# A fused attention and SwiGLU kernel: block 0's output projection moved between block 1's steps, its weights loaded later and in pieces, and two more head pairs turned by DMA

## The chip, the cores and the metric

The kernel runs on one core of one Trainium2 chip. The metric is the time of one execution in device microseconds. The profile takes one execution apart. PE is TensorE (matmuls; PEld are its weight loads), DVE is VectorE, ACT is ScalarE, POOL is GpSimd and SP is SyncE. POOL and SP also issue the DMAs: POOL those that convert float32 in device memory to float16 in SBUF (queue q0), SP the DMA transposes and the stores of the result (queue q1).

## The reference

Attention over 8 batches of 12 heads, 448 tokens each, 64 wide, and then a gated feed-forward network over the 3584 tokens, whose 768 features are the heads side by side:

```python
scores = (q @ k.transpose(0, 1, 3, 2)) / np.sqrt(64)
attn = exp(scores - max(scores));  attn = attn / sum(attn)
x = (attn @ v).transpose(0, 2, 1, 3).reshape(3584, 768)
g, val = x @ w_gate, x @ w_val            # 768 x 1536 each
out = (g * sigmoid(g) * val) @ w_out      # 1536 x 768
```

q, k, v, the weights and the result are float32.

## The kernel before, in words

**Attention.** Two heads are one pair; six pairs are a batch, 48 pairs in all. For each pair the kernel loads q and k (`load_qk16`), brings them into the layout with the feature dimension on partitions (`prep`, giving the tile `qkT`), multiplies them in four units of keys (`qk`, tile `s` in PSUM), lets ScalarE take the exponential (tile `E`), multiplies that with v (`pv`, tile `acc`), and lets VectorE divide by the sums that come along as a 65th column (tile `R`, tile `xt`). `xt` is then turned into the columns of `X` (`turn_x`). v is loaded by `load_v`, three pairs at a time for the first twelve, and copied into its place with the column of ones by VectorE (`copy_v`, tile `vo`).

There are two ways to lay out q and k. Pairs below `NPE` are turned on TensorE by 18 transposing matmuls (the inner function `turn` of `prep`, tile `tp`) and copied out by VectorE. From `NPE` on, POOL copies q and k into the tile `qk16` (three buffers) and SP issues two DMA transposes into `qkT`. Pairs from `QUAD` = 12 on are of another layout with 128 keys to a unit and always go by DMA. For `turn_x`, pairs below `XPE` = 12 use TensorE (tile `xtp`) and a copy by VectorE.

**Feed-forward network.** The tokens come in blocks: block 0 has 384 tokens, block 1 has 512 and so on. A step (`Step`) is one of 12 slices of 128 columns of the gate and value weights: six matmuls for the gate (`gate`, tile `gp`), a tanh on ScalarE (`sg`), a product on VectorE (`gated`, tile `t`), six matmuls for the value (`value`, tile `vp`) and a last product (`finish`, tile `hts`). Weights lie in four parts each (`wg`, `wv`; three steps use one part). The output projection of block 0 is plain: six products of 12 matmuls with 384 columns (`plain_out`, run one at a time by `run_o`, tile `op`), with weights `wo` in two halves, evicted by ScalarE and stored by SP. Later blocks use sums of the weights that VectorE builds from `wo` (`out_sums`), which save matmuls.

**The order.** All instructions are written out by hand in program order (`manual_schedule`), and each engine runs its own in that order. After the first six pairs, whose order is a list of strings, the loop over `plan` makes visits: each visit issues two or three score units, then the products of pairs that are complete (`todo`), and then steps of the network. The number of units is two up to pair `WIDE` and three from there on. How many steps a visit gets is decided in three ways: for the first 12 visits by a budget (`run_budget`, `left`, `carry`), which spreads what is left of the current block by its matmul time up to the next block, for the seven visits ahead of `base` by the list `FIRST_STEPS`, and after that by the table `VISITS`. A turn of `xt` stands at the end of its visit (`turns`). v for the products of a visit is copied one visit earlier (`vcopies`).

**Loads.** `wq` says which loads are emitted when a pair is entered: for example `4: [("g", 3), ("v", 3), ("qk", 12)]` and `6: [("V", 3), ("o", 0)]`. POOL issues them in order. Every DMA has one of eight semaphores in turn, so an issue waits until the DMA eight issues before it has landed. A copy or matmul waits for the semaphores of the loads that it reads.

**PSUM.** The pool `ps_f` has two buffers of one bank (`acc`, `vp`, `xtp` and, in some visits, `gp`), the pool `ps_s` three of two banks (`s`, most `gp`). Buffers are handed out in turn, so an allocation waits for the readers of the one two (or three) before it.

The functions that the change touches:

Of the kernel before, what the change touches and what calls it, by code (L numbers as in the profile page):

```python
# [10 lines left out]
FP32 = mybir.dt.float32  # L11
# [7 lines left out]
GP = 3  # L19
NPE = 12  # L20
LA = 6
RS = 8
RL = 4
FIRST = 6
WIDE = 8
XPE = 12
# [6 lines left out]
QUAD = 12  # L33
# [31 lines left out]
def kernel(  # L65
# [10 lines left out]
    nc = tc.nc  # L76
    B, H, S, D = q.shape
    DM = H * D
    DF = moe_w_gate.shape[1]
# [140 lines left out]
    def load_w(kind, i):  # L220
        if kind == "o":
            src = moe_w_out[:, ts(i, OH)].rearrange("(f p) m -> p f m", p=128)
            dst = wo[i]
        else:
            src = (moe_w_gate if kind == "g" else moe_w_val)[:, ts(i, DF // 4)].rearrange(
                "(t a p) m -> t p a m", p=128, t=2
            )
            for t in range(2):
                nc.gpsimd.dma_start(wgv[kind, i][:, ts(t, NCB // 2), :], src[t])
            return  # L230
        nc.gpsimd.dma_start(dst[:], src)

# [241 lines left out]

    def turn_x(pr):
        b, hp = divmod(pr, NHP)
# [5 lines left out]
        if pr < XPE:  # L482
            tp = accs[pr] if pr < FIRST else ps_f.tile([128, 512], FP32, tag="f", name="xtp")
            for j in range(3):
                nc.tensor.matmul(
                    tp[:, ts(j, 128)],
                    lhsT=xt[:, 2 * j : 2 * j + 2].rearrange("p h d -> p (h d)"),
                    rhs=ident[:],
                    start=True,
                    stop=True,  # L490
                )
            nc.vector.tensor_copy(dst[:, 0:MQ], tp[:, 0:MQ])
            return
# [387 lines left out]
    with tc.manual_schedule():  # L881
# [6 lines left out]
        for vo in Vts:  # L888
# [20 lines left out]
            3: [("qk", 9, 1), ("qk", 10), ("g", 2), ("v", 2)],  # L909
            4: [("g", 3), ("v", 3), ("qk", 12)],  # L910
            6: [("V", 3), ("o", 0)],
            8: [("o", 1)],
        }
# [30 lines left out]

        def add_block(i, visits):
            if i < B - NB - 1:
# [26 lines left out]

        FIRST_STEPS = [2, 2, 1, 2, 1, 1, 1]
        VISITS = [
            (2, 2, 0, 0, 2), (0, 2, 0, 0, 3), (0, 1, 1, 0, 0), (0, 2, 0, 0, 0), (0, 1, 1, 0, 0),
            (0, 2, 0, 0, 0), (0, 1, 1, 0, 0), (0, 2, 0, 0, 0), (0, 1, 1, 0, 0), (3, 2, 0, 0, 1),
            (0, 2, 0, 0, 1), (0, 1, 1, 0, 0), (0, 0, 0, 1, 0), (0, 2, 0, 0, 0), (0, 0, 0, 1, 0),
            (0, 1, 1, 0, 0), (0, 0, 0, 1, 0), (0, 2, 0, 0, 0), (0, 0, 0, 1, 0), (0, 2, 0, 0, 0),
            (4, 2, 0, 0, 1), (0, 2, 0, 0, 1), (0, 1, 1, 0, 0), (0, 1, 0, 0, 0), (0, 1, 1, 0, 0),  # L980
            (0, 1, 0, 0, 0), (0, 1, 1, 0, 0), (0, 1, 0, 0, 0), (0, 1, 1, 0, 0), (0, 1, 0, 0, 0),
            (5, 0, 0, 1, 0), (0, 0, 0, 2, 0), (0, 0, 0, 0, 0),
        ]
# [28 lines left out]

        def run_fv(quiet=False):
            step = fvq.pop(0)
            step.gate()
            step.value(0)
            if not quiet:
                add_sum()
            step.finish()
            if not quiet:  # L1020
                add_sum()
            return 2 * step.time

        def run_pair():
# [30 lines left out]
        def run_o():  # L1055
            gen, t = oq.pop(0)
            next(gen)
            if len(oq) < 2 and not groups and wsums:
                n = 3 if oq else 4
                sums.extend(wsums[:n])  # L1060
                wsums[:n] = []
                add_sum(n)
            return t

# [29 lines left out]
        def run_two_groups(inside=None):  # L1094
            gens = [groups.pop(0)[0]() for _ in range(2)]
            for stage in range(2):
                for gen in gens:
                    next(gen)
                if inside and not stage:
                    inside()  # L1100

        def run_budget(budget):
            while (fvq or oq) and budget > 0:
                if not fvq:
                    budget -= run_o()
                elif len(fvq) > 1 and gate_small[0] and 2 * fvq[0].time < budget:
                    budget -= run_pair()
                elif len(fvq) > 1 and fvq[0].at[1] and 2 * fvq[0].time < budget <= 4 * fvq[0].time:
                    budget -= run_pair()
                else:  # L1110
                    budget -= run_fv(bool(fvq[0].at[1]))
            return budget

        def left():
            return sum(2 * step.time for step in fvq) + sum(t for _, t in oq)

        def share(total, at, n):
            return (at + 1) * total // n - at * total // n

# [56 lines left out]
        turns = []  # L1176

        def open_products(rests):
            for p0 in rests:
                pv_open(p0)  # L1180
                pv_rest(p0)
            return []
# [3 lines left out]

        carry = 0.0
        after_group = False
# [6 lines left out]
        for x, (chunks, todo) in enumerate(plan):  # L1195
# [13 lines left out]
            open_products(rests)  # L1209
            if x == 2:  # L1210
                turn_rests(0)
            end = min([y for y in adds if y > x] + [len(plan) + 1])
            if x == 0:
                add_block(0, end)
            early = [p0 for p0 in vcopies.get(x, []) if p0 < QUAD or x > base]
# [3 lines left out]
            for pr in entered:  # L1219
                lead = [pr + 3] if pr + 3 < QUAD else [pr + 3, pr + 4] if pr + 3 == QUAD else [pr + 4]  # L1220
                for p in lead:
                    if NPE <= p < NPAIR:
                        prep(p)
# [7 lines left out]
            if x in adds and 0 < x < base:  # L1231
                add_block(adds[x], end - x)
            around = bool(todo) and x > base and VISITS[x - base][1:3] == (0, 1)
# [12 lines left out]
            bare = not todo and bool(chunks) and x > 0  # L1246
            if 0 < base - x <= len(FIRST_STEPS):
                n = FIRST_STEPS[x - base]
                gate_small[0] = bare
                if n > 1:  # L1250
                    run_pair()
                else:
                    run_fv(True)
            elif x < base:
                if bare and oq and not fvq:
                    carry -= run_o()
                elif bare:
                    gate_small[0] = True
                out_small[0] = not fvq and bool(oq) and any(p0 >= QUAD for _, p0 in todo)
                extra = 2 * fvq[0].time if bare and len(chunks) == 3 and fvq and not fvq[0].at[1] else 0  # L1260
                carry = run_budget(left() / (end - x) + carry + extra) - extra
            else:
                begins, nf, ng, no, ns = VISITS[x - base]
                gate_small[0] = bare
                if begins > 2:
                    add_block(begins, 0)
                after_group = ng > 0
# [15 lines left out]
                if begins == 2:  # L1283
                    add_block(2, 0)
                ahead = {3: (x + 1, x + 2), 2: (), 1: ()}.get(len(VISITS) + base - x, (x + 1,))
# [71 lines left out]
        p0 = NPAIR - 1  # L1357
        pv_open(p0, True)
        pv_rest(p0)
        pv_quad(p0)  # L1360
# [89 lines left out]
```

## Time and profile before

| | us |
|---|---|
| median of 3 runs (430.68 to 431.16) | 430.89 |
| the profiled execution | 429.48 |
| its span, first to last instruction | 427.7 |
| TensorE busy | 420.7 |
| VectorE, ScalarE, GpSimd busy | 268.8, 245.2, 233.3 |

The lines of the profile give the engine, the kernel's line, the operation, what is written and read, and how often; in a time line the first two numbers are start and length in us, and the bracket at the end is the engine's idle time just before and what ended it. TensorE's matmuls overlap in these lines (the end of one is modelled), so the start of the next line tells how long a group took. A view of windows gives for each stretch its length, the busy time of PE, PEld, DVE, ACT and POOL with the number of instructions, the granted clock as a share of full speed, the DMA engines' busy share and GB/s. In the view of DMA queues the columns are packets, MB and the packets' time as a share of 16 engines; in that of DMA issues the last columns are the count, the size in float16 and the median time from issue to landing.

### The profile page before, as it was taken

How to read it: one execution, taken by the hardware profiler on the slowest of the kernel's cores; microseconds unless marked ns; L12 is line 12 of the kernel's file. 1: busy time of each engine (PE TensorE's matmuls, PEld its weight loads, DVE VectorE, ACT ScalarE, POOL GpSimd, SP SyncE). 2: the span in 40 equal slices, each digit the busy share in tenths (PEclk: the TensorE clock that was granted, in tenths of full speed). 3: DMA queues.
4: the chain of work that ended last, by engine and by line, in shares of the span. 5: the costliest groups of instructions: out<-in, count | busy, mean ns of one | idle time of the engine just before them, and what ended most of it. 6: DMA issues, size and time to landing. Idle time of an engine off the chain costs nothing.

```text
span 427.7 us, 11618 instructions
## 1 busy us (share of the span) xinstructions
PE 420.7 (98%) x4639; PEld 291.0 (68%) x4639; DVE 268.8 (63%) x641; ACT 245.2 (57%) x395; POOL 233.3 (55%) x356
## 2 busy tenths in 40 slices
PE   8999999999999999999999999999999999999995
PEld 4666666655557777757666677777889985555795
DVE  4676572765669665575535786677777755665662
ACT  6976667546755654656666546559654235455221
POOL 8756543988978673577744876925998000000001
PEclk9999999999999999999999999999999999999999
DMA  9999999999999999999999998813101240000124
GB/s 137 179 201 200 200 178 169 127 175 178 154 147 130 127 152 147 142 157 120 130 157 120 160 149 94 138 37 95 23 1 39 76 123 27 0 0 2 38 85 138
DMA packets 107527, 49.77 MB, mean 116 GB/s; under 512 B 59840, under 2 KB 104208, under 8 KB 107472
## 3 DMA queue, kind: packets, MB, share of 16 engines
q0 software_dynamic: 46944, 24.83, 52.9%
q1 hardware_dynamic: 60384, 24.02, 33.6%
q8 instruction: 36, 0.59, 0.6%
q14 instruction: 19, 0.16, 0.1%
q10 hardware_dynamic: 144, 0.17, 0.1%
HBM read 49.55 MB, written 11.01 MB: 142 GB/s over the span
## 4 chain that ended last, share of the span: by engine, by line
PE 84%; DMA 8%; ACT 4%; issue 1%; DVE 1%; POOL 1%; SPq 0%; DVEq 0%; POOLq 0%
PE og L676 18%; PE gp L554 16%; PE vp L554 12%; PE un L792 10%; PE acc L420 8%; PE ub L792 8%; PE s L329 5%; ACT E L367 4%; DMA wo<-in_moe_w_out_dram 4%; DMA qkraw<-in_k_dram 3%; PE op L647 2%; DMA qkT<-qk 1%; PE s L341 1%; PE wp L163 1%; PE op L1000 1%
## 5 line engine op out<-in xcount | busy, mean ns | idle before, releaser
L349 ACT ACTIVATE E<-s 128x896 f16<-128x896 f32 x126 | 106.6, 918 | 40.3 <-PE s L329 28.4
L237 POOL COPY qk<-qkraw 128x512 f16<-128x512 f16 x72 | 45.3, 670 | 53.9 <-DMA qkT<-qk 48.8
L554 PE MATMUL gp<-X,wg 128*128 128x384 f16 (+1 forms) x360 | 73.8, 347 | 0.0
L554 PE MATMUL vp<-X,wv 128*128 128x384 f16 (+3 forms) x360 | 67.7, 324 | 0.0
L607 DVE SCALAR_TENSOR_TENSOR t<-sg,gp 128x384 f32<-128x384 f32 (+1 forms) x60 | 36.3, 607 | 43.0 <-ACT sg L581 42.7
L554 PEld LDWEIGHTS <-wv 128*128 128x128 f16 x450 | 42.9, 98 | 26.0
L637 POOL DMA_DIRECT2D out_dram<-osb x3 | 1.6, 539 | 90.9 <-ACT osb L695 90.9
L554 PEld LDWEIGHTS <-wg 128*128 128x128 f16 x360 | 32.8, 98 | 26.1 <-issue 1.9
L177 POOL DMA_DIRECT2D qkraw<-in_k_dram x70 | 43.0, 637 | 9.4 <-DMA wo<-in_moe_w_out_dram 5.8
L581 ACT ACTIVATE sg<-gp 128x384 f32<-128x384 f32 (+1 forms) x60 | 31.9, 537 | 27.6 <-PE gp L554 26.8
L420 PEld LDWEIGHTS <-E 128*128 128x128 f16 (+1 forms) x1152 | 39.0, 96 | 10.3 <-issue 2.5
L367 ACT ACTIVATE E<-s 112x896 f16<-112x896 f32 x48 | 40.2, 934 | 9.5 <-PE s L359 9.5
L676 PEld LDWEIGHTS <-hts 128*128 128x128 f16 x528 | 44.1, 98 | 0.4
L420 PE MATMUL acc<-vo,E 128*128 128x65 f16 (+1 forms) x1152 | 43.6, 193 | 0.2
L177 POOL DMA_DIRECT2D vraw<-in_v_dram x72 | 43.1, 613 | 0.0
L200 POOL DMA_DIRECT2D qkraw<-in_q_dram x44 | 30.5, 693 | 11.2 <-DMA wo<-in_moe_w_out_dram 6.7
L613 DVE SCALAR_TENSOR_TENSOR hts<-t,vp 128x384 f16<-128x384 f32 (+3 forms) x60 | 32.9, 548 | 5.6 <-PE vp L554 1.9
L695 ACT ACTIVATE osb<-og 128x384 f32<-128x384 f32 x22 | 10.8, 491 | 39.4 <-PE og L676 39.4
L450 DVE TENSOR_TENSOR xt<-acc,R 128x256 f16<-128x256 f32 x72 | 30.6, 425 | 2.5
L329 PE MATMUL s<-qkT 64*128 64x448 f16 x216 | 29.7, 353 | 0.0
L676 PE MATMUL og<-wo,hts 128*128 128x192 f16 x264 | 29.0, 246 | 0.0
L676 PEld LDWEIGHTS <-hsum 128*128 128x128 f16 x300 | 25.5, 98 | 1.0
(179 smaller groups left out, 722.3 us busy)
## 6 DMA issues: line engine op xcount, KB each, us to landing
vraw<-in_v_dram POOLq DMA_DIRECT2D x72, 64.0 KB, 4.0
qkraw<-in_q_dram POOLq DMA_DIRECT2D x41, 112.0 KB, 4.6
qkraw<-in_k_dram POOLq DMA_DIRECT2D x68, 64.0 KB, 4.8
wg<-in_moe_w_gate_dram POOLq DMA_DIRECT2D x8, 288.0 KB, 9.7
wv<-in_moe_w_val_dram POOLq DMA_DIRECT2D x8, 288.0 KB, 10.1
wo<-in_moe_w_out_dram POOLq DMA_DIRECT2D x2, 1152.0 KB, 18.2
out_dram<-osb SPq DMA_DIRECT2D x7, 288.0 KB, 3.8
out_dram<-osb SPq DMA_DIRECT2D x6, 336.0 KB, 3.2
```

The lines of the kernel that those rows point to most:

```text
L177: eng.dma_start(dst[ts(s, 64)], rows)
L237: nc.gpsimd.tensor_copy(dst.rearrange("p c h d -> p h c d"), src)
L329: nc.tensor.matmul(s[:, hx, 0:S], lhsT=t[ts(hx, 64), ts(c + low(pr, hx), 128)], rhs=t[ts(hx, 64), ds(NC * 128, S)], start=True, stop=True,)
L349: nc.scalar.activation(e[:, 0 : 2 * S].rearrange("p (h q) -> p h q", h=2), s[:, :, 0:S], AF.Exp, scale=sm_scale)
L367: nc.scalar.activation(e[:, :, 0:S], s[0:P, :, 0:S], AF.Exp, scale=sm_scale)
L420: nc.tensor.matmul(acc[:, ts(j, D + 1)], lhsT=e[rows, ds(hx * S + j * 128, 128)], rhs=Vts[pr % NV][rows, hx, col, 0 : D + 1], start=first, ...
L554: nc.tensor.matmul(dst[:, 0:w], lhsT=wslice(kind, self.fb, cb), rhs=X[kk][:, cb, ds(c0 + lo, w)], start=(cb == 0), stop=(cb == NCB - 1),)
L581: self.readers = [nc.scalar.activation(self.sg[:, 0:n], gp[:, 0:n], AF.Tanh, scale=0.5)]
L607: nc.vector.scalar_tensor_tensor(self.t1[:, 0:n], self.sg[:, 0:n], 1.0, self.gp[:, 0:n], ALU.add, ALU.mult)
L613: nc.vector.scalar_tensor_tensor(self.hts[:, self.fb, ds(lo, w)], self.t1[:, ds(lo, w)], 0.5 * HS, vp[:, 0:w], ALU.mult, ALU.mult)
L676: nc.tensor.matmul(dst, lhsT=lhs(n), rhs=rhs(n), start=first and n == 0, stop=n == NH - 1, skip_group_check=True)
L792: mm = nc.tensor.matmul(dst, lhsT=lhs[:, n], rhs=rhs[:, n], start=first and n == 0, stop=n == NK - 1, skip_group_check=True,)
```

## The change

1. The output projection of block 0 is moved: its six products no longer stand together in visits 8 to 11, but one each in visits 10, 11, 13, 14, 16 and 17, from visit 11 on inside a step of block 1 (`run_fv_with_o`), between the step's gate and its value, which is then made in two halves.
2. `wo` is loaded when pairs 10 and 12 are entered, instead of 6 and 8, and each half in two pieces of six slices.
3. `NPE` is 10 instead of 12: pairs 10 and 11 are turned by DMA. Which pairs are prepared when is told by a new table, `LEAD`. The load of q and k of pairs 12 and 13 stands ahead of the last quarter of gate and value weights.
4. A table, `FIRST_VISITS`, gives the number of steps and of projection products for each of the first 18 visits, in place of the budget and `FIRST_STEPS`. `WIDE` is 7 instead of 8, so there is one visit less in all, and `VISITS` is written anew: the same 33 entries in another order, but for two single projection products at the end in place of one visit with two and one with none. Block 0's twelve steps are spread over visits 0 to 9.
5. In visits with one step, the turn of `xt` stands inside the step, in the middle of its value group (`run_fv(..., with_turns)`), instead of behind all steps.
6. The last pair's leftover products are issued one visit earlier, and the sums for the later projections are taken two per visit from visit 13 on.

```diff
-NPE = 12
+NPE = 10
-WIDE = 8
+WIDE = 7
...
     def load_w(kind, i):
         if kind == "o":
-            src = moe_w_out[:, ts(i, OH)].rearrange("(f p) m -> p f m", p=128)
-            dst = wo[i]
+            src, n, dst = moe_w_out[:, ts(i, OH)], NFB, wo[i]
         else:
...
+            src, n, dst = (moe_w_gate if kind == "g" else moe_w_val)[:, ts(i, DF // 4)], NCB, wgv[kind, i]
+        src = src.rearrange("(t a p) m -> t p a m", p=128, t=2)
+        for t in range(2):
+            nc.gpsimd.dma_start(dst[:, ts(t, n // 2), :], src[t])
...
-            4: [("g", 3), ("v", 3), ("qk", 12)],
-            6: [("V", 3), ("o", 0)],
-            8: [("o", 1)],
+            4: [("qk", 12), ("g", 3), ("v", 3)],
+            6: [("V", 3)],
+            10: [("o", 0)],
+            12: [("o", 1)],
...
-        FIRST_STEPS = [2, 2, 1, 2, 1, 1, 1]
+        FIRST_VISITS = [
+            (1, 0), (1, 0), (1, 0), (2, 0), (1, 0), (1, 0), (1, 0), (2, 0), (1, 0), (1, 0), (0, 1),
+            (1, 1), (2, 0), (1, 1), (1, 1), (2, 0), (1, 1), (2, 1),
+        ]
...
-        def run_fv(quiet=False):
+        def run_fv(quiet=False, with_turns=False):
             step = fvq.pop(0)
             step.gate()
+            tp = ps_f.tile([128, 512], FP32, tag="f", name="xtp") if turns and with_turns else None
             step.value(0)
+            if tp:
+                step.gated()
+                turn_x(turns.pop(0), tp)
...
+        def run_fv_with_o(quiet):
+            step = fvq.pop(0)
+            step.split = step.alone = True
+            step.gate()
+            step.gated()
+            out_small[0] = True
+            run_o()
+            step.value(0)
+            step.finish()
+            if not quiet:
+                add_sum()
...
+        LEAD = {6: [], 7: [], 8: [10, 11], 9: [12], 10: [13, 14]}
...
             open_products(rests)
-            if x == 2:
+            if (NPAIR - 1, KR - 1) in chunks:
+                pv_open(NPAIR - 1, True)
+                pv_rest(NPAIR - 1)
+            if x == 1:
                 turn_rests(0)
...
-                lead = [pr + 3] if pr + 3 < QUAD else [pr + 3, pr + 4] if pr + 3 == QUAD else [pr + 4]
+                lead = LEAD[pr] if pr in LEAD else [pr + 4]
...
-            if 0 < base - x <= len(FIRST_STEPS):
-                n = FIRST_STEPS[x - base]
+            if x < base:
+                nf, no = FIRST_VISITS[x]
                 gate_small[0] = bare
...
+                if no and not nf:
+                    out_small[0] = True
+                    run_o()
+                elif no:
+                    for _ in range(nf - 1):
+                        run_fv(quiet)
+                    run_fv_with_o(quiet)
+                elif nf > 1:
                     run_pair()
                 else:
-                    run_fv(True)
...
+                    run_fv(quiet, not bare)
+                after_group = no > nf
+                if x > 12:
+                    add_sum(2)
```

## The prediction

> **What bounds the kernel now.** I read the page's busy shares first, then the chain of waits, then the time lines of TensorE, VectorE and GpSimd between 24 and 90 us, where the order of work changes, and the landing times of the loads there.
>
> ```profile
> PE 420.7 (98%) x4639; PEld 291.0 (68%) x4639; DVE 268.8 (63%) x641; ACT 245.2 (57%) x395; POOL 233.3 (55%) x356
> ...
> DMA  9999999999999999999999998813101240000124
> ```
>
> TensorE is busy for 98% of the span, so a microsecond for which it stands still is a microsecond of time. The DMA digits (a slice is 10.7 us) are full up to 256 us: loads come as fast as they can, and their order decides when each lands. The queue that GpSimd feeds, in 35 to 50 us, and then both queues in 57 to 68 us, when DMA transposes have joined:
>
> ```profile
> q0 software_dynamic: 4445, 2.97, 133.3%
> ...
> q0 software_dynamic: 2062, 1.41, 90.5%
> q1 hardware_dynamic: 1970, 0.48, 42.7%
> ```
>
> Alone, the loads (q0) get 4445/15 = 296 packets per us; beside transposes (q1) both get about the same, 187 and 179. So transposes cut the loads to 0.63 of their rate.
>
> The loads that matter, on GpSimd's time line (q and k of pair 9, then v of pairs 9 to 11, then the copies ahead of two pairs' transposes), and their times from issue to landing, from the DMA view of those moments:
>
> ```profile
> 26.36 0.68 POOL L200 DMA_DIRECT2D qkraw<-in_q_dram  x1 [1.03 <-DMA wv<-in_moe_w_val_dram]
> 27.80 0.66 POOL L200 DMA_DIRECT2D qkraw<-in_k_dram  x1 [0.77 <-DMA vraw<-in_v_dram]
> 44.46 0.78 POOL L211 DMA_DIRECT2D vraw<-in_v_dram  x1 [1.13 <-DVE hts L613]
> 52.66 2.28 POOL L237 COPY qk<-qkraw 128x512 f16<-128x512 f16 x4 [0.24 <-DMA qkraw<-in_k_dram]
> ```
> ```profile
> qkraw<-in_k_dram POOLq DMA_DIRECT2D x1, 112.0 KB, 7.9
> vraw<-in_v_dram POOLq DMA_DIRECT2D x1, 336.0 KB, 9.7
> qkT<-qk SPq DMA_TRANSPOSE x1, 8.9
> ```
>
> Pair 9's k lands at 27.80 + 7.9 = 35.7 us; v of pairs 9 to 11 at 44.46 + 9.7 = 54.2. Who needs them, on the time lines of TensorE and VectorE:
>
> ```profile
> 40.80 0.63 PE L302 MATMUL tp<-ident,qkraw 112*64 112x112 f16 x18
> 55.81 0.36 PE L385 MATMUL acc<-vo,E 112*128 112x65 f16 x6
> 56.79 1.14 PE L554 MATMUL gp<-X,wg 128*128 128x384 f16 x6
> 83.22 0.38 PE L341 MATMUL s<-qkT 64*64 64x448 f16 x3 [0.29 <-DMA qkT<-qk]
> ```
> ```profile
> 55.08 0.29 DVE L218 COPY vo<-vraw 112x512 f16<-112x512 f16 x1
> 56.99 0.20 DVE L404 RECIPROCAL R<-acc 128x7 f32<-128x7 f32 x1 [0.41 <-PE acc L393]
> 57.23 0.62 DVE L406 TENSOR_TENSOR xt<-acc,R 128x448 f16<-128x448 f32 x1
> ```
>
> At 40.80 pair 9 is turned, 5.1 us after its k is there. At 55.08 VectorE copies pair 9's v, only 0.9 us after it landed. 55.81 to 56.79 are pair 8's products, and the two rows that follow on VectorE normalise them. At 83.22 stands one of the two waits of TensorE that the profile lists (1.0 and 0.3 us); the other is at the start.
>
> **The change, part by part.** *Moved: block 0's projection and block 1's steps.* The table gives seven steps of block 0 to the first six visits, where the rule gave ten. The work is the same, but pairs now come earlier, while their loads keep their place in a full queue. Up to v of pairs 9 to 11 the queue's content is the same: q and k of pairs 12, 13 pass the last gate and value weights, nothing leaves it, and wo stood behind it anyway. GpSimd issues against landings (the bracketed releasers), not against TensorE. So that v still lands at 54.2 or later.
>
> First wait: the built order of the changed program has pair 9's turn in visit 2. Ahead of it, of what ran before 40.80, three steps are missing (1.95 + 3.90 us), pair 6's products and turn (0.98 + 0.26) and a score unit (0.2): TensorE is there at 40.8 - 7.3 = 33.5 and waits for 35.7, that is 2.2 us.
>
> Second wait: pair 9's v is copied a visit earlier, in visit 5, ahead of pair 8's normalisation in VectorE's order. Ahead of pair 8's products, of what ran before 55.81, four steps are missing (45.64 to 49.54 and 50.55 to 54.46: 7.81 us), the turns of pairs 10 and 11 (0.57 + 0.56) and a score unit (0.2). The products end at 56.79 - 9.1 = 47.7, and the next gate group (0.97) at 48.6, without the first wait. The value group behind it takes the PSUM buffer that pair 8's products hold, so it needs VectorE, which stands at the copy with the normalisation, the gate's product and the next turn's copy queued behind it. ScalarE then runs dry too, as its scores come from TensorE; GpSimd and SP go on.
>
> When does that v land now? GpSimd's copies of pairs 10, 11 (four, 2.3 us) follow its issue at once, so SP starts their transposes near 46.5. Before, the first transpose was issued at 53.30, took 8.9 us to land and has no packet in 50 to 57 us; by that delay of 3.7 us the new ones start at 50.2. The 4.0 us of loads left then take 4.0/0.63 = 6.3: landing at 56.5. Bounds: 54.2 if transposes take nothing, 57.5 if they start at once at 48.5. I take 56.5, as the window of 57 to 68 us is just this mixture. From landing to TensorE: 0.2 to the copy (an estimate; the released steps in the brackets above start within 0.6), 0.29 copy, 0.22 reciprocal with its gap, 0.62 product, 0.1: 1.4 us. TensorE goes on at 57.9 instead of 48.6: **+9.3 us**, the first wait included (bounds 7.0 and 10.3).
>
> *The clock.* TensorE then stands still from 50.8 to 57.9. At the end of the kernel, TensorE's last matmul ends at 422.7, and the granted clock of the next windows is
>
> ```profile
> 422.70:425.70 3.00, 0.00 (x0) 0.00 (x0) 0.36 (x1) 0.03 (x1) 0.00 (x0) 1.00 0.57 177
> 425.70:427.70 2.00, 0.00 (x0) 0.00 (x0) 0.00 (x0) 0.00 (x0) 0.00 (x0) 0.50 0.10 33
> ```
>
> so it halves 3.0 us into a pause. At the start it comes back late:
>
> ```profile
> 0.99 3.38 PE L163 MATMUL wp<-warm 128*128 128x512 f16 x8 [0.99 <-DVE warm L883]
> ...
> 5.19 0.61 PE L163 MATMUL wp<-warm 128*128 128x512 f16 x1
> ...
> 6.30 0.39 PE L163 MATMUL wp<-warm 128*128 128x512 f16 x1
> ```
>
> The matmul at 5.19 is still long, that at 6.30 is not: 4.2 to 5.3 us of work at half speed, half of it lost, 2.1 to 2.6. I take **+2.2**; bounds 0 (the clock holds) and 3.4. The first pause, 2.2 us, is shorter than 3.0, and a loss there would only shorten the second wait. [...] No row here shows a pause of 3 to 7 us in mid-kernel.
>
> *Removed: TensorE's turns of pairs 10 and 11*, 18 small matmuls each, 0.57 + 0.56 = **-1.1**. Instead GpSimd makes four copies (2.3 us) between issues, covered by a queue 9.7 us deep, and SP issues four transposes (1.3 each). A pair is 8 blocks of 112 rows and 64 rows more, 960 packets at 187 per us: pair 10 should land near 50.2 + 5.1 + 1 = 56.3 and is needed at 59.5, pair 11 near 61.5 and needed at 64. The second wait hides them by 2.5 to 3 us; without it they would be the wait.
>
> *Removed: the wait at 83.22*, which the chain traces to wo's load (46.98, 15.24 us): 0.6. The three single steps at 111.68, 116.16 and 120.90 had products of 1.38, 1.51, 1.38 us against 1.14 elsewhere: 0.8. Together **-1.4**. *Moved: wo*, behind pair 14's copies, four issues (about 0.75 each) for two. It should be there near 75; its first product comes at 68.4 + 9.3 = 77.7. Hidden by 2.7 us; without that, it costs what it is late. The sums of wo and the six projection steps with their evictions (0.49) and stores lie on engines with 40% idle.
>
> *Added:* a turn inside a step makes the value group wait for pair products' normalisation: 1.06 us from products' end (56.79 to 57.85, rows above) against 0.97 of gate, 0.15 to 0.3 with the release, in three visits after the wait: **+0.5**. Bounds 0 and 1.0. New neighbours (a score run behind another kind of matmul costs about 0.1): **+0.5**, bounds 0 and 1. Halved value groups cost under 0.1.
>
> Sum on the profiled execution (429.48 us, span 427.7): +9.3 + 2.2 - 1.1 - 1.4 + 0.5 + 0.5 = +10.0, so 439.5. The median of the runs, 430.89, is 1.4 above it: **440.9 us**.
>
> **Rivals.** *The clock holds:* 440.9 - 2.2 = 438.7. For it: no mid-kernel pause is in the trace. Against: the window of 425.70. *A third wait* behind the second: pairs 12 and 13 come a visit after, and their transposes share the queues; pair 13's may land near 70 and are needed at 71.5. If they or wo are 3 us late: 444. For it: before, this chain was late at 83.22. Against: the second wait gives all later loads 9 us. *Faster:* pair 9's v is there when VectorE comes. Then only the small terms are left, -1.5: 429.4. It decides if that v lands within some 1.5 us of 46 us, so below about 48; for it speaks only that the load is re-issued among others, against it 15 us of full queue ahead.
>
> **How the numbers follow.** Forecast 0.54, clock holds 0.2, third wait 0.15, faster 0.07; the other 0.04 are waits so short that the gains about cancel them. The range reaches from 54.2 for the landing with the clock held (430.9 + 7.0 - 1.5 = 436.4, less 0.9 for the added terms at their lower bound) to the third wait with some of the upper bounds: 435.5 to 446. About 0.2% is what a measurement can tell here: faster 0.07, same 0.02, slower 0.91.
>
> **What would show it.** TensorE's weight loads wait about 2 us for pair 9's k near 33 us, and a group near 51 us waits about 7 us for VectorE, whose copy of v waits for its load from 49 us on; the granted clock falls to half after that pause; the wait at 83 us and wo's place in the chain are gone. I am wrong if that v lands before 50 us, or if the copy stands behind the normalisation.

## The result, and the profile after

The changed kernel takes 437.92 us (437.03 to 438.55); the kernel before took 430.78 us on the same chip. The ratio is 1.0166, with a 95% interval of 1.0149 to 1.0183: slower by 7.1 us, where 10.0 were forecast. The profiled execution took 437.9 us with a span of 436.1, 8.4 us more than the span before.

The busy shares and the granted clock on the page of the changed kernel:

```profile
PE 420.1 (96%) x4633; PEld 292.3 (67%) x4633; DVE 263.9 (61%) x644; ACT 244.7 (56%) x395; POOL 235.2 (54%) x362
...
PEclk9999969999999999999999999999999999999999
DMA  9999999999999987899599999544100331000124
```

TensorE's busy time is the same as before, 420 us, in a longer span, and the 6 in the sixth slice says where the clock fell. The four longest waits of TensorE in the changed kernel (total, number, longest, in us):

```profile
PE xtp L481 <- DVE xt L402: 6.2, 1, 6.2
PE tp L298 <- DMA qkraw<-in_k_dram: 1.7, 1, 1.7
PE wp L163 <- DVE warm L879: 1.0, 1, 1.0
PE rtp L504 <- DVE t L603: 0.5, 1, 0.5
```

Before, only the start's wait of 1.0 us and 0.3 us for a transpose were listed. The wait for pair 9's k is the forecast first wait, the one of 6.2 us the second. TensorE's time line around both:

```profile
33.46 0.74 PE L355 MATMUL s<-qkT 64*128 64x448 f16 x6
35.92 0.63 PE L298 MATMUL tp<-ident,qkraw 112*64 112x112 f16 x18 [1.72 <-DMA qkraw<-in_k_dram]
...
49.96 1.14 PE L550 MATMUL gp<-X,wg 128*128 128x384 f16 x6
50.94 0.65 PE L550 MATMUL vp<-X,wv 128*128 128x384 f16 x3
57.75 0.50 PE L481 MATMUL xtp<-ident,xt 128*128 128x128 f16 x3 [6.16 <-DVE xt L402]
58.05 1.17 PE L550 MATMUL vp<-X,wv 128*128 128x384 f16 x3
59.15 1.30 PE L355 MATMUL s<-qkT 64*128 64x448 f16 x6
```

and VectorE's and GpSimd's at the same place, with the load's time to landing from the DMA view of its issue:

```profile
56.63 0.29 DVE L218 COPY vo<-vraw 112x512 f16<-112x512 f16 x1 [7.35 <-DMA vraw<-in_v_dram]
56.84 0.20 DVE L400 RECIPROCAL R<-acc 128x7 f32<-128x7 f32 x1
57.07 0.62 DVE L402 TENSOR_TENSOR xt<-acc,R 128x448 f16<-128x448 f32 x1
```
```profile
44.70 0.81 POOL L211 DMA_DIRECT2D vraw<-in_v_dram  x1 [1.11 <-DVE hts L609]
45.50 2.27 POOL L256 COPY qk<-qkraw 112x512 f16<-112x512 f16 x4
```
```profile
vraw<-in_v_dram POOLq DMA_DIRECT2D x1, 336.0 KB, 11.9
```

The load of v of pairs 9 to 11 is issued at 44.70 us and lands 11.9 us later, at 56.6. VectorE stands 7.35 us at the copy with pair 8's normalisation (the two rows below it) behind it, and TensorE goes on at 57.75 with the turn that needs that normalisation. The clock, in windows of 3.41 us (span, then busy us and number of each engine, granted clock, DMA share, GB/s):

```profile
48.60:52.00 3.40, 2.99 (x47) 1.78 (x43) 0.68 (x2) 2.91 (x4) 3.26 (x6) 1.00 1.31 191
52.00:55.42 3.42, 0.00 (x0) 0.00 (x0) 0.00 (x0) 0.00 (x0) 1.27 (x2) 1.00 1.41 173
55.42:58.83 3.41, 1.08 (x6) 0.60 (x6) 2.03 (x5) 0.00 (x0) 1.39 (x3) 0.50 1.48 143
58.83:62.25 3.42, 3.42 (x41) 2.16 (x40) 0.57 (x2) 2.51 (x3) 1.20 (x3) 0.50 1.72 124
62.25:65.66 3.41, 3.41 (x27) 1.77 (x25) 2.61 (x6) 1.37 (x4) 3.41 (x7) 1.00 1.48 145
```

The queues in 50 to 52 us and in 52 to 56.5, from the DMA view:

```profile
q0 software_dynamic: 502, 0.30, 105.6%
q1 hardware_dynamic: 266, 0.07, 27.0%
```
```profile
q0 software_dynamic: 981, 0.48, 83.8%
q1 hardware_dynamic: 1122, 0.27, 58.8%
```

The transposes (q1) come in after 50 us and then move as many packets as the loads, 249 and 218 per us, so the loads are slowed as forecast, though a little less (187 had been taken).

In the table of windows, half speed lasts from 55.42 to 62.25 us. The work from pair 8's turn to the end of pair 9's products took 57.75 to 62.13, 4.4 us; a visit earlier the same work (47.56 to 49.96) took 2.4. So 2.0 us are the clock's.

The sum over the span: 1.72 + 0.52 + 6.16 of waits, 2.0 of clock, less 1.1 of turns and the 1.4 of waits and slow products that the forecast had as removed, is 7.9 of the 8.4 us measured. (The three products of 1.38 to 1.51 us take 1.14 in the changed kernel, as the others.)

### The profile page after: what moved, and what is told of

Its sections match the earlier page's. It is cut to its first block, busy times and chain, and to the rows that moved or that the text cites. A ratio compares the mean times of both kernels' runs of the same rounds, so it can differ in the third digit from the quotient of the medians.

```text
span 436.1 us, 11628 instructions
## 1 busy us (share of the span) xinstructions
PE 420.1 (96%) x4633; PEld 292.3 (67%) x4633; DVE 263.9 (61%) x644; ACT 244.7 (56%) x395; POOL 235.2 (54%) x362
## 3 DMA queue, kind: packets, MB, share of 16 engines
q1 hardware_dynamic: 62432, 24.52, 31.7%
## 4 chain that ended last, share of the span: by engine, by line
PE 86%; DMA 7%; POOL 3%; DVE 1%; issue 1%; ACT 0%; DVEq 0%; POOLq 0%
PE gp L550 17%; PE og L672 17%; PE vp L550 12%; PE un L788 10%; PE acc L416 8%; PE ub L788 8%; PE s L325 6%; DMA vraw<-in_v_dram 5%; PE op L643 5%; DMA qkraw<-in_k_dram 2%; POOL qkraw L200 2%; PE s L337 1%; PE acc L381 1%; PE op L1001 1%; PE s L355 1%; POOL vraw L211 1%
## 5 line engine op out<-in xcount | busy, mean ns | idle before, releaser
L233 POOL COPY qk<-qkraw 128x512 f16<-128x512 f16 x72 | 43.6, 646 | 66.8 <-DMA qkT<-qk 64.1
L550 PE MATMUL vp<-X,wv 128*128 128x384 f16 (+3 forms) x360 | 66.1, 317 | 0.0
L550 PEld LDWEIGHTS <-wv 128*128 128x128 f16 x480 | 45.6, 98 | 23.2 <-issue 0.2
L416 PE MATMUL acc<-vo,E 128*128 128x65 f16 (+1 forms) x1152 | 42.4, 193 | 0.4 <-DVE hts L609 0.2
L609 DVE SCALAR_TENSOR_TENSOR hts<-t,vp 128x384 f16<-128x384 f32 (+3 forms) x60 | 31.5, 525 | 5.9 <-PE vp L550 3.2
## 6 DMA issues: line engine op xcount, KB each, us to landing
wv<-in_moe_w_val_dram POOLq DMA_DIRECT2D x8, 288.0 KB, 10.2
```

Source lines behind the costliest of these rows:

```text
L233: nc.gpsimd.tensor_copy(dst.rearrange("p c h d -> p h c d"), src)
L416: nc.tensor.matmul(acc[:, ts(j, D + 1)], lhsT=e[rows, ds(hx * S + j * 128, 128)], rhs=Vts[pr % NV][rows, hx, col, 0 : D + 1], start=first, ...
L550: nc.tensor.matmul(dst[:, 0:w], lhsT=wslice(kind, self.fb, cb), rhs=X[kk][:, cb, ds(c0 + lo, w)], start=(cb == 0), stop=(cb == NCB - 1),)
```

## The experiments

All edits are to the changed kernel. Each ratio is against the kernel before on the same chip.

**Only the late load.** v of pairs 9 to 11 is issued earlier:

```diff
-            4: [("qk", 12), ("g", 3), ("v", 3)],
-            6: [("V", 3)],
+            4: [("V", 3), ("qk", 12), ("g", 3), ("v", 3)],
```

> The changed kernel, with the load of v of pairs 9 to 11 issued ahead of q and k of pairs 12, 13 and of the last gate and value weights, nothing else moved. My theory: that v lands near 46 us instead of 56.6 and VectorE's copy waits for nothing, but most of the gain is lost at once: TensorE then stands at the first scores of pair 10, which it reaches near 52.3 us and whose DMA transposes still land at 57.4 and 57.9 us, as the same issues stand ahead of GpSimd's copies for them. It goes on 1.2 us earlier than before at these scores (57.9 for 59.15), and the clock still halves in a pause of 5.6 us: 436.7 us (436 to 437.5). Rival: the late v is the only cause and the transposes come in time once VectorE is not held up; then the wait of 6.2 us and the slow stretch of 2.0 us are both gone: 429.7 us.

437.83 us, ratio 1.0162 (1.0122 to 1.0202): no gain that can be measured. The load now lands at 46.0 us, and VectorE waits for it no more. On TensorE's time line the wait stands at pair 10's scores instead:

```profile
57.65 0.93 PE L355 MATMUL s<-qkT 64*128 64x448 f16 x4 [3.73 <-DMA qkT<-qk]
```

The rival (429.7) falls. The 1.2 us that I had expected came and went again. TensorE goes on with pair 10's scores at 57.65 us, 1.5 us earlier than in the changed kernel (59.15), but from there it works for 6.3 us at half speed, where the changed kernel had 3.1 us left:

```profile
57.18:60.59 3.41, 2.94 (x38) 2.05 (x39) 0.00 (x0) 2.35 (x3) 1.41 (x3) 0.50 1.50 124
60.59:64.01 3.42, 3.42 (x18) 1.87 (x16) 1.38 (x3) 0.67 (x2) 2.77 (x5) 0.50 2.08 160
```

At the next scores the two are level (64.50 us here, 64.40 there). The clock also fell behind the *first* wait, of 1.8 us:

```profile
33.29:36.70 3.41, 1.61 (x31) 0.86 (x30) 0.95 (x3) 2.53 (x3) 2.28 (x3) 1.00 1.43 197
36.70:40.11 3.41, 3.41 (x39) 2.40 (x37) 1.44 (x3) 0.00 (x0) 2.01 (x5) 0.50 1.33 203
```

So TensorE came to the scores at 53.9 and not at 52.3; that shortened the wait there, but not the time at which it ends, which the transposes set.

**Only the transposes.** Pairs 10 and 11 turned by TensorE:

```diff
-NPE = 10
+NPE = 12
-        LEAD = {6: [], 7: [], 8: [10, 11], 9: [12], 10: [13, 14]}
+        LEAD = {6: [], 7: [], 8: [], 9: [12], 10: [13, 14]}
```

> The changed kernel, with pairs 10 and 11 turned by TensorE again and not by DMA; loads and steps as in the changed kernel. My theory: the four transposes took part of the DMA engines from the load of v of pairs 9 to 11, so without them it lands at about 54.3 us, as in the kernel before, and not at 56.6; TensorE goes on at 55.5 us instead of 57.75, and the 1.1 us of turns lie inside the pause, which is then about 3 us long. If the clock holds through such a pause the 2.0 us of slow work are gone too: 433.6 us; if it halves, 435.6. Rival: the transposes have no part in it and v lands at 56.6 us all the same: 437.9 us, or up to 439 with the turns on the path.

437.15 us, ratio 1.0149 (1.0127 to 1.0171). Issued at 46.01 us, the load of v took 9.7 us to land, as in the kernel before, and not 11.9: the transposes do cost it 2.2 us. But in this run the queue was late: this load was issued 1.3 us later, and the first wait was 2.6 us (a run with turns by DMA has 2.6 us there too, and one with this edit 1.5, so that isn't the edit's). So the load landed at 55.7 and TensorE went on at 56.67, only 1.1 us earlier than in the changed kernel, and with half a value group still to do, as pair 11's turn held the PSUM buffer that the value group needs:

```profile
51.90 1.14 PE L550 MATMUL gp<-X,wg 128*128 128x384 f16 x6
56.67 1.12 PE L550 MATMUL vp<-X,wv 128*128 128x384 f16 x3 [3.63 <-DVE qkT L299]
```

A pause of 3.6 us halved the clock too, for one window of 3.41 us (56.42 to 59.83) and not two. The rival on the landing falls; my 433.6 to 435.6 was too low.

**Both edits together.**

> Both edits: v of pairs 9 to 11 loaded earlier, and pairs 10, 11 turned by TensorE. My theory: neither the copy of v nor the scores of pair 10 wait, so the pause of 6.2 us and the slow stretch of 2.0 us go and the turns' 1.1 us come back: 437.9 - 6.2 - 2.0 + 1.1 = 430.8 us, plus what the next late load costs, as TensorE then needs pair 12's transposes near 62 and the output weights near 72 us, which landed at 62.9 and 76.8 in the changed kernel: 430.8 to 435. Rival: the queue is behind as a whole, and a third wait takes the full 7 us again: 437.

433.07 us, ratio 1.0055 (1.0039 to 1.0071). As forecast, neither the copy nor the scores wait; of TensorE's waits the first one is left, with a window at half speed behind it (37.87 to 41.28 us):

```profile
PE tp L298 <- DMA qkraw<-in_k_dram: 2.9, 1, 2.9
...
PE acc L381 <- DVE vo L218: 0.3, 1, 0.3
PE op L643 <- DMA wo<-in_moe_w_out_dram: 0.2, 1, 0.2
```

Two edits that gain 0.1 and 0.8 us alone gain 4.9 together (medians): the late v and the late transposes stand one behind the other, and either hides the other. The last line also shows the next one, the output weights, now late by 0.2 us.

**The place of the copy in VectorE's order,** with pairs 10, 11 turned by TensorE:

```diff
-            early = [p0 for p0 in vcopies.get(x, []) if p0 < QUAD or x > base]
+            early = [p0 for p0 in vcopies.get(x, []) if p0 < QUAD and p0 != 9 or x > base]
```

> Pairs 10, 11 turned by TensorE (as in the run with that edit alone, 437.15 us) and VectorE's copy of pair 9's v put behind pair 8's normalisation, all loads as changed. My theory: the copy holds VectorE as long as before, but pair 8 is normalised first, so TensorE goes on through the value group, a turn and pair 10's scores, some 2 to 2.5 us of work, until pair 9's products need the copy: the wait of 3.8 us shrinks to 1 to 2 and the clock holds: 432.5 to 434.5 us. Rival: the place of the copy does not matter, because the gated product and the cast of the turn stand behind it anyway: 437 us.

433.65 us, ratio 1.0092 (1.0069 to 1.0114), by the ratios 2.5 us less than with the turns alone. VectorE waits for the same load, but pair 8 is normalised before it:

```profile
51.73 0.62 DVE L402 TENSOR_TENSOR xt<-acc,R 128x448 f16<-128x448 f32 x1
55.18 0.29 DVE L218 COPY vo<-vraw 112x512 f16<-112x512 f16 x1 [2.82 <-DMA vraw<-in_v_dram]
55.39 0.55 DVE L603 SCALAR_TENSOR_TENSOR t<-sg,gp 128x384 f32<-128x384 f32 x1
```

TensorE waits 1.9 and 0.8 us instead of 3.6, and the clock stays at 1.00, where the run with the turns alone did 3.15 us of work at half speed. The shorter waits make 0.9 of the 2.5 us, the clock most of the rest. So it was what stood queued behind the copy that stopped TensorE, not only the load.

**The first wait alone.** Pair 9's q and k are loaded with pair 8's:

```diff
-            1: [("V", 2), ("qk", 8, 1), ("g", 1), ("v", 1)],
-            3: [("qk", 9, 1), ("qk", 10), ("g", 2), ("v", 2)],
+            1: [("V", 2), ("qk", 8), ("g", 1), ("v", 1)],
+            3: [("qk", 10), ("g", 2), ("v", 2)],
```

> The changed kernel with q and k of pair 9 loaded together with pair 8's, ahead of the second gate and value weights, nothing else moved. My theory: the first wait (1.7 to 2.9 us near 34 us) goes, but TensorE only comes that much earlier to the second, which still ends with v of pairs 9 to 11 at 56.6 us: 437.9 us, as changed. Rival: each wait costs on its own, and the time falls by the first one: 436 us.

437.82 us, ratio 1.0150 (1.0133 to 1.0167). The first wait is gone and the second is longer by about what was gained:

```profile
57.58 0.50 PE L481 MATMUL xtp<-ident,xt 128*128 128x128 f16 x3 [7.68 <-DVE xt L402]
```

**The clock.** 24 matmuls that nothing reads, in the pause:

```diff
                 step.gated()
+                if turns[0] == 8:
+                    for _ in range(24):
+                        nc.tensor.matmul(step.spare, lhsT=warm[:], rhs=warm4, start=True, stop=True)
                 turn_x(turns.pop(0), tp)
```

> The changed kernel, with 24 matmuls of 512 columns on constant data (0.21 us each, 5.1 us in all, into a PSUM bank that nothing reads) put into the pause of TensorE in visit 5, ahead of pair 8's turn. My theory: with work in the pause the granted clock stays full, and the stretch from that turn to the end of pair 9's products takes 2.4 us, as the same work did a visit before, and not 4.4: 437.9 - 2.0 = 435.9 us. Rival: the dip costs nothing, because a later load holds TensorE up anyway: 437.9 us.

443.83 us, ratio 1.0305: the matmuls, which write the second bank of the gate's tile, waited for VectorE's reader of the first (a wait of 4.7 us at L1023) and ran after the pause, on the path. That says nothing on the theory. With the two banks declared independent:

> The changed kernel with 24 matmuls of 512 columns in TensorE's pause of visit 5, now free of any order against VectorE's and ScalarE's readers of the tile's other bank (in the run before they stood behind VectorE's gated product and ran after the pause). My theory: the clock stays full behind the pause, and the 4.4 us from pair 8's turn to the end of pair 9's products take 2.4: 437.9 - 2.0 = 435.9 us. Rival: the slow stretch costs nothing, as a later load holds TensorE up: 437.9 us.

434.95 us, ratio 1.0125 (1.0098 to 1.0152); by the ratios 1.8 us less than the changed kernel, though the intervals just touch (1.0149 to 1.0183 there). The time lines settle it. TensorE's:

```profile
51.11 5.34 PE L1023 MATMUL gp<-warm 128*128 128x512 f16 x24
57.62 0.34 PE L481 MATMUL xtp<-ident,xt 128*128 128x128 f16 x3 [1.17 <-DVE xt L402]
...
58.42 0.74 PE L355 MATMUL s<-qkT 64*128 64x448 f16 x6
```

The turn is released at the same moment (57.62 for 57.75), the clock is 1.00 throughout, and the scores take 0.74 us and not 1.30. At the first step of block 1 this run is 2.1 us ahead of the changed kernel (81.02 for 83.14 us). The 2.0 us of the clock are a cost by themselves.

**The table.** Ten steps in the first five visits, as the rule before had it, and none in visits 7 to 9:

```diff
-            (1, 0), (1, 0), (1, 0), (2, 0), (1, 0), (1, 0), (1, 0), (2, 0), (1, 0), (1, 0), (0, 1),
+            (2, 0), (2, 0), (2, 0), (2, 0), (2, 0), (1, 0), (1, 0), (0, 0), (0, 0), (0, 0), (0, 1),
```

(A visit with neither a step nor a projection issues nothing there.)

> The changed kernel, with the first visits' table set so that ten of block 0's twelve steps come in the first five visits, as the rule of the kernel before had it, two more in visits 5 and 6, and none in visits 7 to 9; loads, turns and output weights as changed. My theory: the table is what brought TensorE ahead of the loads, so with four steps more (7.8 us) ahead of pair 8's products both waits near 34 and 51 us shrink to under 1.5 us in all and the clock stays full, which gives back 6.5 to 8 us and 2 us; the three visits without a step then run at ScalarE's pace and lose 1 us each: 437.9 - 9 + 3 = 432 us (430 to 434). Rival: the loads' places and the transposes decide alone, whatever the table: 437.9 us or more.

436.75 us, ratio 1.0167 (1.0124 to 1.0211). Half of the theory held: both waits are gone, and VectorE's copy, at 56.25, waits 0.74 us, which costs nothing:

```profile
56.25 0.29 DVE L218 COPY vo<-vraw 112x512 f16<-112x512 f16 x1 [0.74 <-DMA vraw<-in_v_dram]
```

The other half was mis-sized: the visits without a step cost far more than 3 us, as the clock fell there as well, though no single wait on TensorE is longer than 1 us:

```profile
63.85 0.36 PE L355 MATMUL s<-qkT 64*128 64x448 f16 x2 [0.63 <-ACT E L363]
...
65.46 0.36 PE L325 MATMUL s<-qkT 64*128 64x448 f16 x2 [0.44 <-ACT E L363]
```
```profile
64.15:67.56 3.41, 1.86 (x38) 1.28 (x35) 0.59 (x2) 3.41 (x5) 3.41 (x6) 1.00 1.11 158
67.56:70.97 3.41, 3.11 (x35) 1.81 (x36) 0.80 (x2) 2.31 (x4) 3.41 (x7) 0.50 1.11 138
70.97:74.38 3.41, 2.45 (x29) 1.41 (x26) 1.98 (x4) 1.27 (x2) 2.53 (x5) 0.50 1.28 156
74.38:77.79 3.41, 3.41 (x47) 2.47 (x42) 1.26 (x5) 1.75 (x3) 0.59 (x1) 0.50 1.29 176
```

So the table did bring TensorE ahead of the loads. Of the two orders tried, each covers one stretch with the twelve steps and leaves the other bare.

**Towards a version without waits.** Pairs 10, 11 turned by TensorE, and the loads in another order:

```diff
-            1: [("V", 2), ("qk", 8, 1), ("g", 1), ("v", 1)],
-            3: [("qk", 9, 1), ("qk", 10), ("g", 2), ("v", 2)],
+            1: [("V", 2), ("qk", 8), ("g", 1), ("v", 1)],
+            3: [("qk", 10), ("V", 3), ("g", 2), ("v", 2)],
             4: [("qk", 12), ("g", 3), ("v", 3)],
-            6: [("V", 3)],
-            10: [("o", 0)],
+            9: [("o", 0)],
```

> The changed kernel with pairs 10, 11 turned by TensorE, q and k of pair 9 loaded with pair 8's, v of pairs 9 to 11 ahead of the third gate and value weights, and the first half of the output weights one entry earlier. My theory: against the run with v early and the turns (433.07 us) the wait of 2.9 us for pair 9's k and the slow clock behind it (3.6 us at half speed, 1.7 us) go too, and no other load becomes late: 428.5 us (427.5 to 431), faster than both kernels. Rival: the queue is full, and what comes 4.6 us earlier now waits for the third gate weights or the output weights: 432 to 434 us.

436.60 us, ratio 1.0160 (1.0127 to 1.0193). All waits for loads up to 64 us are gone, and a new one takes their place, which neither theory had named:

```profile
70.70 0.58 PE L337 MATMUL s<-qkT 64*64 64x448 f16 x3 [6.31 <-DMA qkT<-qk]
```

Pair 13's copies now stood behind the issue of the output weights on GpSimd, so its transposes were issued at 59.9 and 61.2 us and landed at 68.9 and 70.7. With `9: [12, 13], 10: [14]` in the table of leads they go ahead of it:

> The kernel of the run with all loads early (436.6 us), with GpSimd's copies for pair 13's transposes put ahead of the issue of the output weights, with pair 12's, instead of behind it. My theory: in that run the one wait left was for pair 13's transposes (6.3 us at 70.7), which were issued near 60 us behind the output weights and shared the queues with them; issued near 53 they land by 63, and the output weights land near 70 as TensorE comes for them: the wait of 6.3 us and the slow clock behind it (6.8 us at half speed, some 3 us) go: 428 us (427 to 430), faster than both kernels. Rival: the transposes are late because the queues carry too much at that time, whatever the order, and the wait moves to the output weights: 432 us or more.

431.13 us, ratio 1.0007 (0.9980 to 1.0034): the whole loss is made good, but no gain is shown. The profiled execution, of 429.25 us, has no load among TensorE's waits (one each of 0.5, 0.3 and 0.2 us beside the start). Its ten executions reach from 429.25 to 433.52, with mean granted clocks of 0.998 to 0.993; what is late in the longer ones isn't in the one trace that there is.

**The output weights earlier still,** ahead of pair 12's v and pair 15's q and k:

> The last kernel (all loads early, pair 13's copies first: 431.13 us, its runs between 429.25 and 433.52), with the output weights issued one place earlier still, right behind pair 13's copies and ahead of v of pair 12 and q and k of pair 15. My theory: the runs near 432.5 us are those in which a load with less than 1 us to spare (the output weights landed at 69.58 us and are needed near 70) came late and the clock fell; with 3 us more to spare for the output weights most runs come near 429.5: 429.5 to 430.2 us, ahead of the kernel before by some 0.2%. Rival: another load is the narrow one (v of pair 12, or pair 14's transposes, which come later now): 431 to 433 us.

433.10 us, ratio 1.0063 (1.0039 to 1.0087): worse, as the rival said, though through pairs 12 and 13: their transposes now share the queue with the output weights, and land late.

```profile
PE s L337 <- DMA qkT<-qk: 1.6, 1, 1.6
...
PE s L325 <- DMA qkT<-qk: 0.6, 1, 0.6
```

The trace is of an execution of 431.27 us, near the fastest; its 2.2 us of waits are what it lies above the profiled execution of the version before (429.25). What made others longer, up to 436.15 us, isn't in it.

**The transposes of pairs 10, 11 alone,** put back into the version at 431.13 us (`NPE = 10`, `8: [10, 11]`):

> The last kernel (all loads early, pair 13's copies first: 431.13 us), with pairs 10 and 11 turned by DMA again, as the change has it. My theory: this part alone brings the loss back: the transposes can be issued only when GpSimd comes to their copies behind the last weights' issue, near 47 us, and land near 57, while TensorE, which now waits for nothing before, wants pair 10's scores near 50 us: a wait of 7 us and 6.8 us at half speed behind it, less the 1.1 us of turns: 437 to 439 us. Rival: with every other load early they land in time, and only the 1.1 us of TensorE's turns are saved: 430 us.

438.18 us, ratio 1.0169 (1.0149 to 1.0190):

```profile
58.24 1.30 PE L355 MATMUL s<-qkT 64*128 64x448 f16 x6 [7.87 <-DMA qkT<-qk]
```

Issued at 47.13 and 48.53 us, pair 10's land at 57.2 and 58.1, where TensorE is there at 50.4. This one part of the change costs 7 us by itself as soon as nothing else hides it.

## Why the prediction was right, and where it was off

The forecast mechanism is the one that happened, in all steps but one.

*First wait:* 2.2 us forecast, 1.72 measured. That it "would only shorten the second wait" is shown by the run without it: 437.82 us.

*Second wait.* v of pairs 9 to 11 was to land at 56.5 us; it landed at 56.60. The transposes' share in that was right: 11.9 us to landing with them, 9.7 without. That VectorE's order holds the normalisation behind the copy is shown by the run with the copy moved. TensorE went on at 57.75 for a forecast 57.9. The term of +9.3 us measured 8.4 (1.72 + 0.52 + 6.16, where the 0.52 are a wait at L504 that I had not listed). The step that failed is "The value group behind it takes the PSUM buffer that pair 8's products hold": its first half ran at 50.94, before pair 8 was normalised, and only the turn waited. The program asks for the turn's buffer ahead of the value group's, so with buffers handed out in that order the value group would have had pair 8's. As it ran before VectorE had read that one, it had the other. That is 0.5 of the 0.9 us; the rest is a resume that was 0.15 us earlier and an arrival 0.25 us later than worked out.

*Clock:* +2.2 forecast, 2.0 measured, and the run with matmuls in the pause shows it as a cost of its own. No run shows the forecast's upper bound of 3.4 us; what the changed kernel shows is the 2.0. The rival in which the clock holds falls. But "The first pause, 2.2 us, is shorter than 3.0, and a loss there would only shorten the second wait" held in its first half where the clock stayed at 1.00 behind that pause, in the changed kernel (1.72 us) and with the turns alone (2.6), but not in all: in three of the runs a wait of 1.8 to 2.9 us there (1.8 with v loaded early, 2.6 with the matmuls behind VectorE's reader, 2.9 with both edits) was followed by a window of 3.41 us at half speed. That "it halves 3.0 us into a pause" is what the end of the kernel before shows and no more: in these runs the clock halved 3.8 us into the pause (the changed kernel), 3.4 (turns alone), 3.1 (pair 9's k early) and 4.5 (loads in another order). The size differed too: 4.5 us of work were done at half speed in the changed kernel, 6.3 with v loaded early.

*Removed:* TensorE's wait near 83 us is gone from the list of waits (its row gave 0.29 us where the forecast took 0.6), and the output weights landed at 76.8 us for a first product at 79.40, hidden by 2.6 us where 2.7 were forecast. The turns are gone from TensorE's rows; their transposes landed at 57.9 and 61.3 us (forecast 56.3 and 61.5, with 960 packets for a pair; the page counts 62432 in q1 for 60384 before, 1024 for each of the two) and were not waited for; pair 10's had 1.2 us to spare.

*Added:* "a turn inside a step makes the value group wait for pair products' normalisation", +0.5, did not happen: behind pair 7's products the gate group starts at 46.10 and the value group at 47.08, 0.98 us later, as without a turn. It has the same cause as the step above: the value group had the other PSUM buffer. Where pair 11's turn takes that one (the run with the turns alone), it does wait for VectorE, 3.63 us. The +0.5 for new neighbours was measured by no run; it is as large as what the sum of the rest lacks (7.9 for 8.4).

So 10.0 - 0.9 - 0.5 - 0.2 = 8.4 us between the two profiled executions. The rest of the difference to 440.9 is the offset: the profiled execution before lay 1.4 us below its median, the one after on it, so "the median of the runs, 430.89, is 1.4 above it" did not carry over.

One bound doesn't follow from the working's own numbers, which changed nothing: transposes that start at once start near 46.5 us, not 48.5, and then the landing would be 58.7 and not 57.5.

*Rivals.* The third wait did not come in the changed kernel, but it stood near: once nothing held TensorE before, the output weights were late by 0.2 us (both edits) and pair 13's transposes by 6.3 (loads in another order). The price of the rival *faster*, 429.4 us if pair 9's v is there when VectorE comes, was wrong: that case was built, and it takes 437.83 us, as pair 10's transposes are then the wait. I had the row for it ("The second wait hides them by 2.5 to 3 us; without it they would be the wait") and did not use it in the rival. The price also left out the first wait, which is part of the +9.3 us and stays when v comes in time: with the transposes out of the way as well, it is what remains, and the time is 433.07 us.

What stays open is whether the new order can beat the kernel before: the best version is even with it (1.0007), and the narrow load in its longer executions was not found. The 0.5 us that the sum lacks are not explained either.

## What to carry to other kernels

Where loads fill the queue and an order is written out by hand, moving work away from in front of a pair is the same as asking for that pair's loads earlier: list every load's landing against its new first use, and not only the first that is late, for the next stands hidden behind it and gives the whole loss back when the first is mended (0.1 and 0.8 us for either edit alone, 4.9 for both). Where an engine works through its instructions in order, as VectorE did here (a wait of 7.35 us with the normalisation behind it), a copy that waits for a load belongs behind the work that others wait for; that was worth 2.5 us, the clock included, without moving a load.

## What the hardware showed beyond the forecast

The clock fell without a long pause. Half speed lasted 3.41 us with the turns alone, 6.83 in the changed kernel and 10.2 with the table. In the window of 3.41 us ahead of it TensorE had been busy for 1.61 us beside a single wait of 1.8 us (v loaded early, from 36.70 us on), and for 1.86 us beside waits of under 1 us, with many of the matmuls there of 65 columns (the table, from 67.56 on). A window with 1.66 us of work (the run with turns alone, 32.53 to 35.94) was not followed by half speed, so busy time as these rows give it isn't all that counted. Nor is the length of a wait: those of 1.7 us (the changed kernel) and 2.6 us (turns alone) were followed by a clock of 1.00, the one of 1.8 us by 0.50. Full speed came back behind windows with 3.15 us of work (turns alone), 3.41 (v loaded early, the table) and 3.42 (the changed kernel); in the run with the table 3.11 and 2.45 us were followed by another window at half speed.

The transposes issued while the queue of loads was full took long to land: 8.7 to 10.7 us in the changed kernel for the six of pairs 10 to 12, issued from 46.7 us on, and 4.9 and 5.4 us for pair 13's, issued at 58.7 and 60.0 us, when GpSimd had issued a single load since 55.
